# Attention scores of two heads on the two halves of the TensorE array, in a fused attention and mixture kernel

## The chip, the core and the metric

The kernel runs as one program on one core of a Trainium2 chip. The metric is the device time of that program in microseconds (us). The engines are named as the profile names them: PE (TensorE, the matrix array) with PEld for its weight loads, DVE (VectorE), ACT (ScalarE), POOL (GpSimd) and SP (SyncE, which issues the transfers).

## What is computed

Attention with a block mask feeds a first mixture layer, which feeds a second one. The change is in the attention alone, and there almost wholly in `scores = scale * q @ k.T`:

```python
B, H, S, D = 4, 8, 576, 64                  # batches, heads, positions, head width
scores = scale * np.matmul(q, k.transpose(0, 1, 3, 2))
scores = np.where(pos[:, None] // 64 >= pos[None, :] // 64, scores, -1e9)
attn = softmax(scores)                      # max taken off, sum + 1e-9
x = np.matmul(attn, v)                      # heads side by side: (2304, 512)
x = maximum(x @ w1, x @ w2, x @ w3) @ w_out # first mixture layer, d_ff 768
out = sum_e p[:, e] * (maximum(x @ W1[e], 0) @ W2[e])   # second, 4 experts, d_ff 1024
```

All inputs are 32-bit floats, and the products must be more exact than one pass of the array in its rounded 32-bit form (`F32R`) gives. So a factor is held as two parts, the rounded value ("high") and what is left of it ("low"), and several products of parts are summed.

## The kernel before

**Stages.** There are 16 pairs of heads, four to a batch. Batch 0's attention runs by itself; from then on the first mixture layer of batch b (`moe1`, matmuls on line 528) is mixed into the attention of batch b + 1 as filler, and what is left of it runs on after the last scores, until about 530 us. The second mixture layer (lines 883 to 1042) takes the rest of the time and isn't touched by the change.

**Order of the work.** The loop in `program` writes the stages of one head after another (scores, transposes of the probabilities, products with v, filler). The instructions of each engine are then put in order once, when the program is built, by a scheduler that plans with a model of the engines; on the chip every engine takes its own instructions in that fixed order. The `order` fences below show that order.

**Loads and preparation.** `load_pair` (line 89) brings queries and keys of a pair with each head's 64 rows held twice, on partitions 0 to 63 and again on 64 to 127: 2 x 2 x 576 columns. `prep_pair` (line 105) makes the parts. Keys: ACT rounds 1152 columns (line 85), and DVE takes the rounded value off on the lower 64 partitions (line 122), so that `kk` holds high parts on top and low parts below. Queries: ACT scales and rounds 1024 and 128 columns (line 133) into `q1`, DVE forms the low parts `q2` (line 135). POOL clears a 64-column gap in each (line 118). In batch 0 the odd pairs put all this in `spare`.

**Scores.** `scores` (line 163) makes one head's scores in two groups. For query block i (128 queries) the key widths are 128, 256, 384 and 512. A block takes two matmuls of 128 array rows (line 190): `kk` against `q1`, which sums high x high and low x high, and against `q2`. The last 64 queries of both heads make one further block (i = 4, 320 and 256 columns) of four matmuls each. In batches 0 and 1 one short matmul with `corner` (line 195) masks a block; in batches 2 and 3 DVE does (line 204). Then DVE finds the extreme of each row (line 208), ACT takes the exponential (line 215), `normalise` makes reciprocals (lines 223, 224). The scores' PSUM tiles come from `ps_x`, four banks that `tt` (transposes, line 274) and others use too, and `ps_c`.

**Around it.** `turn_probs` transposes probabilities on PE (line 274) and copies them out (DVE or ACT, line 299). In batch 0 the values (line 328) are 32-bit matmuls without parts.

Of the kernel before, what the change touches and what calls it, by code (L numbers as in the profile page):

```python
# [24 lines left out]
def program(tc, q, k, v, w123, w_out, probs, e_w1, e_w2, out):  # L25
    nc = tc.nc

    B, H, D, S = q.shape[0], 2 * q.shape[1], q.shape[2] // 2, q.shape[4]
# [25 lines left out]
    nc.gpsimd.memset(corner[0:1, 0:64], 1e15)  # L54
# [26 lines left out]
    QT, QW = 2 * (S - 64), 2 * S + 64  # L81
    pairs, heads, later, made = {}, {}, [], {}
# [6 lines left out]
    def load_pair(g):  # L89
        b, h0 = divmod(2 * g, H)  # L90

        if g % 2:
            raw = ap_.tile([P, 2, 2, S], F32, name="raw", tag="raw")[:]
        else:
            o = (B - 1) * KD * S
            raw = arena[:, o:o + 4 * S].rearrange("p (n h s) -> p n h s", n=2, h=2)
        for hs in ((0, 1), (1, 2)) if g == 0 else ((0, 2),):
            for n, src in ((1, k), (0, q)):
                nc.sync.dma_start(out=raw[:, n, hs[0]:hs[1]], in_=src[b, h0 // 2, :, hs[0]:hs[1]])

        vraw = ap_.tile([P, 5, 2, D], F32, name="vraw", tag="vraw", bufs=4)
        nc.sync.dma_start(out=vraw, in_=v[b, h0 // 2])
        pairs[g] = dict(raw=raw, vraw=vraw)

    def prep_pair(g):


        raw, vraw = pairs[g]["raw"], pairs[g]["vraw"]
        if g < NPAIR and g % 2:

            spare = mp.tile([P, 2 * QW + 2 * S], F32R, name="spare", tag="hh")
            q1, q2 = spare[:, 0:QW], spare[:, QW:2 * QW]
            kk = spare[:, 2 * QW:].rearrange("x (h s) -> x h s", h=2)
        else:
            q1, q2 = (ap_.tile([P, QW], F32R, name=x, tag=x, bufs=1)[:] for x in ("q1", "q2"))
            kk = ap_.tile([P, 2, S], F32R, name="kk", tag="kk", bufs=1)[:]
        for x in (q1, q2):
            nc.gpsimd.memset(x[:, QT + 64:QT + 128].bitcast(U32), 0)

        def keys(hs):  # L120
            (rounded if g else lambda _, to, x: rounded(nc.vector, to, x))(nc.scalar, kk[:, hs], raw[:, 1, hs])
            nc.vector.tensor_tensor(kk[hi, hs], raw[hi, 1, hs], f(kk[hi, hs]), op=ALU.subtract)

        def queries(hs):
            x = raw[:, 0, hs]
            parts = []
            for to in (q1, q2):
                main = to[:, 0:QT].rearrange("x (h s) -> x h s", h=2)[:, hs]
                tail = to[:, QT:QW].rearrange("x (t s) -> x t s", s=64)[:, 0:3:2][:, hs]
                parts.append((main, tail))  # L130
            srcs = (x[:, :, 0:S - 64], x[:, :, S - 64:S])
            for high, src in zip(parts[0], srcs):
                nc.scalar.activation(high, src, ACTF.Copy, scale=-scale)  # L133
            for high, low, src in zip(*parts, srcs):
                nc.vector.scalar_tensor_tensor(low, src, -scale, f(high), op0=ALU.mult, op1=ALU.subtract)

        if g == 0:
            for h in range(2):
                keys(slice(h, h + 1))
                queries(slice(h, h + 1))  # L140
            yield
        else:
            keys(slice(0, 2))
            yield
            queries(slice(0, 2))
        pairs[g].update(q1=q1, q2=q2, kk=kk)
        if g < NPAIR:
# [6 lines left out]
        pairs[g]["vs"] = vs  # L154
# [3 lines left out]
    GROUPS = [  # L158
        [("x", 512, [(0, 0, P), (2, P, 384)]), ("x", 512, [(3, 0, 512)])],
        [[("x", 512, [(1, 0, 256)])], [("c", 1024, [(4, 192, 576), (1, 768, 256)])]],  # L160
    ]

    def scores(g, grp):
        pair, h = pairs[g // 2], g % 2
        if grp == 0:
            heads[g] = dict(
                p=[None] * 4,
                mn=ap_.tile([P, 5], F32, name="mn", tag="mn", bufs=3),
                sm=ap_.tile([P, 5, 2], F32, name="sm", tag="sm", bufs=3),
            )  # L170
        mn, sm, pt = heads[g]["mn"], heads[g]["sm"][:, :, 0], heads[g]["p"]
        masked = g < 2 * H
        c0 = 3 * grp
        sets = []
        for tag, cols, plan in GROUPS[1][h] if grp else GROUPS[0]:
            st = (ps_x if tag == "x" else ps_c).tile([P, cols], F32, name="st", tag=tag)
            sets.append((st, plan))
            for i, o, w in plan:

                if i == 4:  # L180
                    todo = [(QT + 64 * x, x) for x in range(2)]
                else:
                    todo = [(h * QT // 2 + P * i, h)]
                c = 0
                while c < w:
                    n = min(w - c, 512 - (o + c) % 512)
                    terms = [(part, q0, x) for q0, x in todo for part in ("q1", "q2")]
                    ends = masked and i < 4 and c + n == w
                    for m, (part, q0, x) in enumerate(terms):
                        nc.tensor.matmul(  # L190
                            out=st[:, o + c:o + c + n], lhsT=pair[part][:, q0:q0 + P],
                            rhs=pair["kk"][:, x, c:c + n], start=m == 0, stop=m == len(terms) - 1 and not ends,
                        )
                    if ends:
                        nc.tensor.matmul(  # L195
                            out=st[:, o + w - 64:o + w], lhsT=corner, rhs=corner[:, 0:64], start=False, stop=True
                        )
                    c += n
        c = c0
        done = []  # L200
        for st, plan in sets:
            for i, o, w in plan:
                if i < 4 and not masked:
                    nc.vector.memset(st[lo, o + w - 64:o + w], 1e30)
            mine = [(c + n, *x) for n, x in enumerate(plan)]
            c += len(plan)
            for col, i, o, w in mine:
                nc.vector.tensor_reduce(mn[:, col:col + 1], st[:, o:o + w], axis=AX.X, op=ALU.min)  # L208
            for col, i, o, w in mine:
                x = ap_.tile([P, w], F32, name=f"p{i}", tag=f"p{i}", bufs=2 if i == 4 else 3)  # L210
                if i == 4:
                    pair["p4"] = x
                else:
                    pt[i] = x
                nc.scalar.activation(  # L215
                    x, st[:, o:o + w], ACTF.Exp, bias=mn[:, col:col + 1], scale=-1.0,
                    accum_out=sm[:, col:col + 1],
                )
                done.append((col, x))

        def normalise():
            cs = slice(c0, c)
            nc.vector.tensor_scalar(sm[:, cs], sm[:, cs], 1e-9, None, op0=ALU.add)
            nc.vector.reciprocal(sm[:, cs], sm[:, cs])  # L224
            if g < H:

                if grp == 0 and h == 0:
                    o = 4 * (g // 2) * P
                    pair["rb"] = arena[:, o:o + 4 * P].rearrange("p (i h c) -> p i h c", i=4, h=2)
                rb = pair["rb"][:, 0:3, h] if grp == 0 else pair["rb"][:, 3:4, h]  # L230
                rs = sm[:, c0:c] if grp == 0 else sm[:, c - 1:c]
                nc.gpsimd.tensor_copy(rb, rs.unsqueeze(2).to_broadcast([P, c - c0 if grp == 0 else 1, 64]))
            for col, x in done:
                if g < H and x is not pair.get("p4"):
                    continue
                nc.gpsimd.tensor_scalar(x, x, sm[:, col:col + 1], 1.0, op0=ALU.mult, op1=ALU.mult)  # L236
# [22 lines left out]
    def turn_probs(g, part):  # L259
# [8 lines left out]
        pt = heads[g]["p"] + [pair["p4"]]  # L268
# [42 lines left out]
    def values32(g, part):  # L311


        pair, hd, h = pairs[g // 2], heads[g], g % 2
        eh, vraw = pair["eh"], pair["vraw"]
        own = lo if h == 0 else hi
# [21 lines left out]
        if part == 0:  # L338
            nc.scalar.copy(xf[own, 0:P], hd["pv"][0][own, 0:P])
# [7 lines left out]
        del heads[g]  # L347
# [12 lines left out]
    def values(g, part):  # L360
# [3 lines left out]
        hd, vs, h = heads[g], pairs[g // 2]["vs"], g % 2  # L364
# [23 lines left out]
        own, other = (lo, hi) if h == 0 else (hi, lo)  # L388
# [6 lines left out]
        tmp = ap_.tile([P, 512], F32, name="tmp", tag="tmp", bufs=1)[own, 0:n]  # L395
# [972 lines left out]
```

## Time and profile before

| | |
|---|---|
| three timed runs | 1253.21, 1253.94, 1254.67 us; median 1253.94 |
| span of the profiled execution | 1247.6 us (first to last instruction), 6.3 us under the median |
| PE busy | 1210.9 us, 97% of the span |
| DVE, ACT, POOL busy | 934.0, 516.4, 339.0 us |
| attention | from 0 to about 400 us |

The page's granted TensorE clock is 9 or more tenths of full speed in all 40 slices. PE is the engine with the most work over the whole span; the first 88 us, batch 0, differ from the rest, and so a change is to be weighed stage by stage. Matmul durations in the trace include the time in which a matmul runs out of the array while the next one is already in it; what a matmul costs in a full stretch is the distance from its start to the next one's.

### The profile page before, as it was taken

Reading aid. Unit: us, or ns where it says so; the run is one execution under the profiler, and the core shown is the slowest. Engines: PE = TensorE matmul, PEld = TensorE weight load, DVE = VectorE, ACT = ScalarE, POOL = GpSimd, SP = SyncE. Lnnn points to the kernel's source line nnn. Section 1 sums busy time; section 2 is a strip of 40 time slices with the busy share of each in tenths; the row PEclk is TensorE's granted clock in tenths of the full one; section 3 lists DMA queues with packets and bytes.
Section 4 is the critical chain, followed back from the end, with each engine's and each line's share of the span. In section 5 each row is a group of like instructions: output and inputs, shape, how many; then the busy total and the mean of one; then the engine's idle time right before and its main releaser. Section 6 shows DMA issues by size and latency. Waiting matters only on the chain.

```text
span 1247.6 us, 19748 instructions
## 1 busy us (share of the span) xinstructions
PE 1210.9 (97%) x7433; PEld 1157.6 (93%) x7433; DVE 934.0 (75%) x1720; ACT 516.4 (41%) x1076; POOL 339.0 (27%) x428
## 2 busy tenths in 40 slices
PE   6889998999999999999999999999999999999998
PEld 5668997999999999989999998999999999999998
DVE  8979888666565634378888886758787788586896
ACT  7976767544544421234434441233232222322232
POOL 3648786454344212243333341000000000000000
PEclk9999999999999999999999999999999999999999
DMA  8745475545533488479888865778787887766754
GB/s 320 266 144 194 162 263 167 168 151 156 182 103 118 120 298 293 154 305 336 306 308 297 312 239 169 281 279 317 294 310 308 313 315 289 253 251 235 253 203 178
DMA packets 82644, 299.69 MB, mean 240 GB/s; under 512 B 8748, under 2 KB 18036, under 8 KB 69492
## 3 DMA queue, kind: packets, MB, share of 16 engines
q1 hardware_dynamic: 82548, 298.42, 67.2%
q8 instruction: 59, 0.97, 0.3%
q14 instruction: 37, 0.30, 0.1%
HBM read 215.26 MB, written 83.14 MB: 239 GB/s over the span
## 4 chain that ended last, share of the span: by engine, by line
PE 71%; DVE 13%; DMA 7%; ACT 4%; issue 3%; POOL 2%; SPq 0%; DVEq 0%; ACTq 0%; POOLq 0%
PE m L883 22%; PE m L528 19%; PE o L1042 17%; DMA t<-in_e_w 3%; PE st L190 3%; PE pv L382 2%; PE tt L274 2%; PE m L1042 2%; DMA part<-in_e_w 2%; DVE mn L208 2%; PE o L965 1%; PE o L968 1%; PE o L969 1%; PE pv L328 1%; DVE w L838 1%
## 5 line engine op out<-in xcount | busy, mean ns | idle before, releaser
L528 PE MATMUL m<-xh,wt 128*128 128x288 f32 x1120 | 238.8, 298 | 1.9 <-DVE mt L566 1.6
L883 PE MATMUL m<-t,w 128*128 128x384 f32 x1152 | 228.5, 336 | 0.0
L1042 PE MATMUL o<-hx,w 128*128 128x384 f32 x1176 | 225.8, 337 | 0.0
L1042 PEld LDWEIGHTS o<-hx,w 128*128 128x128 f32 x1176 | 207.9, 188 | 0.0
L883 PEld LDWEIGHTS m<-t,w 128*128 128x128 f32 x1152 | 203.3, 188 | 2.6 <-DVE tmp L903 0.4
L528 PEld LDWEIGHTS m<-xh,wt 128*128 128x128 f32 x1120 | 183.8, 188 | 2.8 <-DVE mt L566 2.0
L883 PE MATMUL m<-b,w 128*128 128x384 f32 x864 | 175.7, 337 | 2.9 <-ACT tmp L908 2.9
L528 PE MATMUL m<-xl,wt 128*128 128x288 f32 x560 | 165.2, 295 | 0.0
L883 PEld LDWEIGHTS m<-b,w 128*128 128x128 f32 x864 | 153.2, 188 | 6.0 <-ACT tmp L908 3.2
L528 PEld LDWEIGHTS m<-xl,wt 128*128 128x128 f32 x560 | 105.2, 188 | 0.3
L903 DVE TENSOR_TENSOR tmp<-m,tmp 128x384 f32<-128x384 f32 x144 | 77.8, 549 | 18.7 <-PE m L883 18.3
L236 POOL TENSOR_SCALAR p<-p,sm 128x128 f32<-128x128 f32 (+4 forms) x112 | 73.7, 674 | 46.5 <-DVE sm L224 17.5
L528 PE MATMUL m<-hh,wo 128*128 128x288 f32 x384 | 81.3, 299 | 2.7 <-ACT arena L577 1.3
L215 ACT ACTIVATE p<-st,mn 128x128 f32<-128x128 f32 (+3 forms) x144 | 78.4, 554 | 8.3 <-DVE mn L208 7.8
L1013 ACT CAST hx<-hq 128x768 fp32r<-128x768 f32 x49 | 40.5, 836 | 99.2 <-PE o L1042 76.1
L190 PE MATMUL st<-kk,q 128*128 128x128 f32 (+4 forms) x336 | 70.3, 339 | 7.5 <-ACT q L133 5.3
L965 PE MATMUL o<-w,hh 128*128 128x512 f32 x192 | 74.7, 391 | 0.8 <-ACT hh L943 0.5
L968 PE MATMUL o<-w,hh 128*128 128x512 f32 x192 | 74.7, 390 | 0.0
L969 PE MATMUL o<-w,hl 128*128 128x512 f32 x192 | 74.1, 390 | 0.0
L838 POOL TENSOR_TENSOR w<-part,w 128x512 fp32r<-128x512 f32 x32 | 48.8, 1547 | 88.7 <-ACT w L836 71.3
L566 DVE TENSOR_TENSOR mt<-m,mt 128x288 f32<-128x288 f32 x96 | 43.1, 452 | 39.1 <-PE m L528 38.6
L208 DVE TENSOR_REDUCE mn<-st 128x1 f32<-128x128 f32 (+3 forms) x144 | 66.4, 504 | 2.8 <-PE st L195 2.5
(173 smaller groups left out, 2182.0 us busy)
## 6 DMA issues: line engine op xcount, KB each, us to landing
w<-kb SPq DMA_DIRECT2D x55, 1024.0 KB, 5.5
w<-ka SPq DMA_DIRECT2D x30, 1792.0 KB, 7.5
ka<-w SPq DMA_DIRECT2D x16, 1792.0 KB, 6.7
wt<-held SPq DMA_DIRECT2D x54, 512.0 KB, 4.1
kb<-part SPq DMA_DIRECT2D x16, 1024.0 KB, 6.9
kb<-w SPq DMA_DIRECT2D x16, 768.0 KB, 5.2
arena<-in_w SPq DMA_DIRECT2D x18, 512.0 KB, 4.1
wo<-held SPq DMA_DIRECT2D x12, 768.0 KB, 4.5
```

The source lines that it names most:

```text
L190: nc.tensor.matmul(out=st[:, o + c:o + c + n], lhsT=pair[part][:, q0:q0 + P], rhs=pair["kk"][:, x, c:c + n], start=m == 0, stop=m == len(t ...
L208: nc.vector.tensor_reduce(mn[:, col:col + 1], st[:, o:o + w], axis=AX.X, op=ALU.min)
L215: nc.scalar.activation(x, st[:, o:o + w], ACTF.Exp, bias=mn[:, col:col + 1], scale=-1.0, accum_out=sm[:, col:col + 1],)
L236: nc.gpsimd.tensor_scalar(x, x, sm[:, col:col + 1], 1.0, op0=ALU.mult, op1=ALU.mult)
L528: nc.tensor.matmul(out=out_, lhsT=w, rhs=x, start=m == 0, stop=m == n - 1)
L838: eng.tensor_tensor(w[:, a:b, 1], raw[:, a:b], f(w[:, a:b, 0]), op=ALU.subtract)
L883: ins = nc.tensor.matmul(out=m, lhsT=a, rhs=b, start=start and n == 0, stop=stop and n == 3 * KH - 1, skip_group_check=True,)
L903: nc.vector.tensor_tensor(t, x, y, op=ALU.add)
L965: ins = nc.tensor.matmul(out=o, lhsT=hh[:, ts], rhs=wh, start=i == 0, stop=False)
L968: nc.tensor.matmul(out=o, lhsT=hh[:, ts], rhs=wl, start=False, stop=False)
L969: nc.tensor.matmul(out=o, lhsT=hl[:, ts], rhs=wh, start=False, stop=i == G - 1)
L1042: nc.tensor.matmul(out=o, lhsT=a, rhs=b, start=start and m == 0, stop=stop and m == 2, skip_group_check=True,)
```

## The change

Queries and keys of a pair are now held once: head 0 on partitions 0 to 63, head 1 on 64 to 127. A score matmul uses half of the array's rows (64 of 128), and the matmuls of the two heads are written alternately, into different PSUM tiles. Since high and low parts can no longer be stacked on the array's rows, a block takes three matmuls a head (high x high, high x low, low x high; `TERMS`); low x low is left out. The last 64 queries lie in the same columns for both heads, with zeros laid in by the host, so that their block is three matmuls of all 128 rows (line 176). Scores come in three stages a pair; the loop goes over pairs; `qk` has two buffers where `q1`, `q2`, `kk` had one.

```diff
-            raw = ap_.tile([P, 2, 2, S], F32, name="raw", tag="raw")[:]
+            raw = ap_.tile([P, S + QW], F32, name="raw", tag="raw")[:]
...
+        nc.sync.dma_start(out=raw[:, 0:S], in_=k[b, m])
+        nc.sync.dma_start(out=raw[:, S:], in_=q[b, m])
...
+            spare = ap_.tile([P, 2 * (S + QW)], F32R, name="qk", tag="qk", bufs=2)
-        for x in (q1, q2):
-            nc.gpsimd.memset(x[:, QT + 64:QT + 128].bitcast(U32), 0)
...
-            nc.vector.tensor_tensor(kk[hi, hs], raw[hi, 1, hs], f(kk[hi, hs]), op=ALU.subtract)
+        rounded(nc.scalar if n else nc.vector, ks[0], raw[:, 0:S])
+        nc.vector.tensor_tensor(ks[1], raw[:, 0:S], f(ks[0]), op=ALU.subtract)
+        yield
+        nc.scalar.activation(qs[0], raw[:, S:], ACTF.Copy, scale=-scale)
+        nc.vector.scalar_tensor_tensor(qs[1], raw[:, S:], -scale, f(qs[0]), op0=ALU.mult, op1=ALU.subtract)
...
+    STEPS = [
+        (("x", 512), ("x", 512), [(0, 0, 0, P), (2, P, P, 384)]),
+        (("x", 512), ("x", 512), [(3, 0, 0, 512)]),
+        (("x", 512), ("c", 1024), [(1, 0, 768, 256)]),
     ]
+    TERMS = ((0, 0), (0, 1), (1, 0))
...
-                    terms = [(part, q0, x) for q0, x in todo for part in ("q1", "q2")]
...
+            for m, (x, y) in enumerate(TERMS):
+                for h in range(2):
+                    nc.tensor.matmul(
+                        out=views[h], lhsT=qs[x][own[h], P * i:P * i + P], rhs=ks[y][own[h], 0:w],
+                        start=m == 0, stop=m == 2 and not masked,
+                    )
...
+        if step == 2:
+            view = st[1][:, 192:768]
+            for c, n_ in ((0, 320), (320, 256)):
+                for m, (x, y) in enumerate(TERMS):
+                    nc.tensor.matmul(
+                        out=view[:, c:c + n_], lhsT=qs[x][:, QT:QW], rhs=ks[y][:, c:c + n_],
+                        start=m == 0, stop=m == 2,
+                    )
...
-            todo = [ta, s0, tb, s1, pp, va, pp, vb]
+        todo = [ta[0], s0, tb[0], s1, va[0], pp, vb[0], ta[1], s2, tb[1], va[1], pp, vb[1]]
```

**Order on PE, in the third batch.** `st` is a scores tile, `m` the filler's, `tt` a transpose's. Before, one head's scores of blocks 0, 2 and 3:

```order
L528 MATMUL m_3532<-xl_2461,wt_3530 128x288
L528 MATMUL m_3532<-xh_2460,wt_3530 128x288
L274 MATMUL tt_3622<-ident_58,p2_3272 128x128
L190 MATMUL st_3649<-kk_3338,q1_3336 128x128
L190 MATMUL st_3649<-kk_3338,q2_3337 128x128
L190 MATMUL st_3649<-kk_3338,q1_3336 128x384
L190 MATMUL st_3649<-kk_3338,q2_3337 128x384
L190 MATMUL st_3654<-kk_3338,q1_3336 128x512
L190 MATMUL st_3654<-kk_3338,q2_3337 128x512
```

Now, of a pair in the same batch, where `st_3789` and `st_3871` are head 0's and `st_3790` and `st_3872` head 1's:

```order
L510 MATMUL m_3772<-xh_2386,wt_3722 128x288
L161 MATMUL st_3789<-qk_3549 128x128 x3
L161 MATMUL st_3789<-qk_3549 128x384 x3
L161 MATMUL st_3790<-qk_3549 128x128 x3
L161 MATMUL st_3790<-qk_3549 128x384 x3
L510 MATMUL m_3821<-xh_2386,wt_3819 128x288
...
L161 MATMUL st_3871<-qk_3549 128x512 x3
L510 MATMUL m_3889<-xh_2386,wt_3887 128x288
...
L161 MATMUL st_3872<-qk_3549 128x512 x3
```

The three terms of a block stand together, first all of one head, then all of the other; the alternation of the source is kept in few places.

**Order on DVE, in batch 0.** The preparation of one later pair and the copy of transposed probabilities, `eh`, behind it. Before:

```order
L135 SCALAR_TENSOR_TENSOR q_634<-arena,q_633 128x1024
L135 SCALAR_TENSOR_TENSOR q_634<-arena,q_633 128x2x64
L122 TENSOR_TENSOR kk<-arena,kk 64x1152
L299 COPY eh<-tt 128x512
L223 TENSOR_SCALAR sm<-sm 128x3
```

Now:

```order
L118 TENSOR_TENSOR qk<-raw,qk 128x576
L444 SCALAR_TENSOR_TENSOR arena<-arena 128x512
L121 SCALAR_TENSOR_TENSOR qk<-raw,qk 128x640
L203 TENSOR_SCALAR sm<-sm 128x3
L204 RECIPROCAL sm<-sm 128x3
L282 COPY eh<-tt 128x512
```

The preparation of a pair is two instructions of 576 and 640 columns where it was three of 1152, 1024 and 128.

**Order on DVE, at the start of the program.** Before:

```order
L135 SCALAR_TENSOR_TENSOR q_132<-arena,q_131 128x512
L135 SCALAR_TENSOR_TENSOR q_132<-arena,q_131 128x64
L208 TENSOR_REDUCE mn<-st 128x1 x4
L122 TENSOR_TENSOR spare<-raw,spare 64x1152
L208 TENSOR_REDUCE mn<-st 128x1 x2
```

Now:

```order
L121 SCALAR_TENSOR_TENSOR qk<-arena,qk 128x640
L118 TENSOR_TENSOR spare<-raw,spare 128x576
L121 SCALAR_TENSOR_TENSOR spare<-raw,spare 128x640
L118 TENSOR_TENSOR qk<-arena,qk 128x576
L189 TENSOR_REDUCE mn<-st 128x1 x6
```

The first reductions of scores now stand behind the preparation of the second pair and the keys of the third.

## Rows read from the trace of the kernel before

**Rows 1.** The page's first line: span and instructions of the profiled execution.

```profile
span 1247.6 us, 19748 instructions
```

**Rows 2.** Stretches: length, each engine's busy us (instructions), granted clock, DMA share, GB/s.

```profile
core 0: us, PE busy (x) PEld busy (x) DVE busy (x) ACT busy (x) POOL busy (x), PEclk, DMA share, GB/s
0.00:88.00 88.00, 68.97 (x384) 51.68 (x384) 75.56 (x150) 72.99 (x191) 44.40 (x71) 0.96 0.73 257
88.00:240.00 152.00, 144.36 (x1052) 136.56 (x1052) 127.79 (x291) 102.36 (x250) 105.47 (x137) 1.00 0.57 190
240.00:520.00 280.00, 277.90 (x2073) 274.70 (x2072) 155.79 (x387) 115.02 (x282) 95.90 (x156) 1.00 0.54 172
```

**Rows 3.** PE's waits, 0 to 88 us: total us, times, longest.

```profile
PE st L190 <- ACT q L133: 5.3, 1, 5.3
PE pv L328 <- ACT eh L299: 4.8, 2, 2.5
PE tt L274 <- DVE eh L299: 2.3, 1, 2.3
```

**Rows 4.** The chain that ended last, by line, 0 to 88 us.

```profile
by line: PE pv L328 12.4%; DVE mn L208 10.0%; issue 8.4%; DVE q L135 5.9%; PE st L190 5.5%; DVE kk L122 4.8%; ACT p L215 4.5%; DVE spare L135 4.4%; DMA arena<-in_q 3.9%; DVE eh L299 3.5%; PE tt L274 3.5%; DVE spare L122 3.3%; ACT spare L85 
```

**Rows 5.** Timeline, DVE and PE around 50 us: start, length, instructions, idle before.

```profile
47.63 2.50 DVE L135 SCALAR_TENSOR_TENSOR q<-arena,q 128x1024 fp32r<-128x1024 f32 x2
50.16 2.60 DVE L122 TENSOR_TENSOR kk<-arena,kk 64x1152 fp32r<-64x1152 f32 x1
52.79 0.69 DVE L299 COPY eh<-tt 128x512 f32<-128x512 f32 x1
...
53.54 0.65 PE L274 MATMUL tt<-ident,p 128*128 128x128 f32 x4 [2.27 <-DVE eh L299]
```

**Rows 6.** Timeline of PE in full stretches, at 304 and 313 us.

```profile
304.72 0.52 PE L190 MATMUL st<-kk,q 128*128 128x256 f32 x3
305.08 0.60 PE L274 MATMUL tt<-ident,p 128*128 128x128 f32 x4
305.44 1.29 PE L190 MATMUL st<-kk,q 128*128 128x128 f32 x6
306.57 0.29 PE L528 MATMUL m<-xh,wt 128*128 128x288 f32 x1
306.70 0.29 PE L528 MATMUL m<-xl,wt 128*128 128x288 f32 x1
...
313.01 1.46 PE L190 MATMUL st<-kk,q 128*128 128x320 f32 x10
314.30 0.29 PE L528 MATMUL m<-hl,wo 128*128 128x288 f32 x1
```

**Rows 7.** Timeline of PE, two scores of 128 columns and a corner.

```profile
49.74 0.42 PE L190 MATMUL st<-spare 128*128 128x128 f32 x2
49.99 0.20 PE L195 MATMUL st<-corner 128*128 128x64 bf16 x1
```

**Rows 8.** Busy time of DVE's line 122 alone, 0 to 88 us.

```profile
0.00:88.00 88.00, 9.99 (x7) 0.96 0.73 257
```

**Rows 9.** Busy time of DVE's line 135 alone, 0 to 88 us.

```profile
0.00:88.00 88.00, 11.57 (x14) 0.96 0.73 257
```

**Rows 10.** Groups by line and shape, 0 to 88 us: count, busy us, mean ns.

```profile
L547 DVE TENSOR_TENSOR xl<-xf,xh 128x576 fp32r<-128x576 f32 x4 | 3.3, 830 | 0.0
L135 DVE SCALAR_TENSOR_TENSOR q<-arena,q 128x512 fp32r<-128x512 f32 x2 | 1.4, 692 | 0.2 <-ACT q L133 0.2
L85 ACT CAST kk<-arena 128x1152 fp32r<-128x1152 f32 x2 | 2.3, 1147 | 0.0
L546 ACT CAST xh<-xf 128x576 fp32r<-128x576 f32 x4 | 2.7, 678 | 0.3 <-DVE xf L358 0.3
```

**Rows 11.** The first 10 us, as in rows 2.

```profile
0.00:10.00 10.00, 4.66 (x19) 3.77 (x19) 5.58 (x12) 3.91 (x10) 1.27 (x12) 1.00 0.82 292
```

**Rows 12.** The chain in order of time: the first reductions.

```profile
8.16 0.68 DVE mn L208 x2
```

More of the change, by code (lines that the diff above doesn't have):

```diff
@@ L79, in program @@
     lo, hi, both = slice(0, 64), slice(64, 128), slice(0, P)
-    QT, QW = 2 * (S - 64), 2 * S + 64
-    pairs, heads, later, made = {}, {}, [], {}
+    own = (lo, hi)
+    QT, QW = S - 64, S + 64
+    pairs, later, made = {}, [], {}
     def rounded(engine, to, x):
@@ L153, in prep_pair @@
         nc.gpsimd.tensor_tensor(vs[:, :, :, 64:128], src, f(vh), op=ALU.subtract)
[L154 to L160, printed above, removed]
-    ]
[L163 to L169, printed above, removed]
-            )
[L171 to L178, printed above, removed]
+        pairs[n]["vs"] = vs
@@ L180, in scores @@
                 if i == 4:
-                    todo = [(QT + 64 * x, x) for x in range(2)]
+                    pair["p4"] = to
                 else:
[L183 to L186, printed above, removed]
-                    terms = [(part, q0, x) for q0, x in todo for part in ("q1", "q2")]
[L188 to L214, printed above, removed]
+                    pair["p"][h][i] = to
@@ L233, in normalise @@
-            for col, x in done:
-                if g < H and x is not pair.get("p4"):
+                    to = pair["rb"][:, 0:2].rearrange("p i h c -> p h i c")
+                    rs = sm[:, cs].rearrange("p (h i) -> p h i", h=2).unsqueeze(3).to_broadcast([P, 2, 2, 64])
+                else:
+                    to = pair["rb"][:, step + 1]
+                    rs = sm[:, COLS[step]:COLS[step] + 2].unsqueeze(2).to_broadcast([P, 2, 64])
+                nc.gpsimd.tensor_copy(to, rs)
+            for c, i, x in done:
+                if n < NPAIR and i < 4:
@@ L267, in turn_probs @@
         el = eh[:, LAST + 2:]
-        pt = heads[g]["p"] + [pair["p4"]]
+        pt = pair["p"][h] + [pair["p4"]]
         for n in PARTS[part]:
@@ L311, in values32 @@
     def values32(g, part):
-        pair, hd, h = pairs[g // 2], heads[g], g % 2
+        pair, h = pairs[g // 2], g % 2
+        hd = pair.setdefault(h, {})
         eh, vraw = pair["eh"], pair["vraw"]
-        own = lo if h == 0 else hi
+        mine = own[h]
         both_v = [vraw[:, j].rearrange("p h d -> p (h d)") for j in range(5)]
@@ new lines, in program @@
+    for n in range(NALL):
+        b, d = divmod(n, NPAIR)
+        ahead = n + 2 < NALL
+        prep = prep_pair(n + 2) if ahead else iter(())
+        g = 2 * n
+        ta, tb, va, vb = [
+            [(fn, g + h, part) for h in range(2)] for fn in (turn_probs, values) for part in range(2)
+        ]
+        s0, s1, s2 = [(scores, n + 1, i) if n + 1 < NALL else (None,) for i in range(3)]
+        pp = (next, prep, None)
+        todo = [ta[0], s0, tb[0], s1, va[0], pp, vb[0], ta[1], s2, tb[1], va[1], pp, vb[1]]
+        for m, st in enumerate(todo):
+            if d == NPAIR - 1 and m == 7:
+                moe1_inputs(b, range(KD - 1))
+            stage(*st)
+            if b == 0 and st is vb[0] and n:
+                weigh(n - 1, made["pv"])
+            if d == NPAIR - 1 and m == len(todo) - 1:
+                if b == 0:
+                    weigh(n, made["pv"])
```

179 lines of the change are left out of this document (82 added, 97 removed).

## The prediction

> **What bounds the kernel now.** I first read the line with the span [rows 1] and the table of stretches [rows 2]. From 240 to 520 us PE is busy 277.9 of 280 us while DVE has 155.8: there every nanosecond on PE is on the path, and DVE, ACT and the loads are cover. From 88 to 240 us PE is busy 144.4 of 152 us, so 7.6 us are stalls. From 0 to 88 us (batch 0) PE is busy 69.0 of 88, DVE 75.6 and ACT 73.0: no engine is full, work passes from one to the next, and 19.0 us are stalls of PE. PE's waits say for whom [rows 3]: 5.3 us is the start, before the first queries are ready, and nearly all the rest ends with ACT's or DVE's copy of transposed probabilities (line 299). The chain of waits in that stretch [rows 4] says why these are late: DVE's preparation of later pairs (lines 135 and 122) is 5.9 + 4.8 + 4.4 + 3.3 = 18.4% of it, 16.2 us. One place shows it plainly [rows 5]: DVE spends 5.1 us from 47.6 us on a later pair's query and key parts, only then makes the copy, and PE sits idle 2.27 us for it. After 520 us nothing of the change is left.
>
> So there are two accounts: what the change takes off DVE and ACT counts in the first 88 us and for some of the 7.6 us after them; what it adds to PE counts nearly in full from 88 us on.
>
> **PE's scores.** What a matmul costs is the distance between starts in a full stretch [rows 6]. Three of 256 columns: 304.72 to 305.08, 0.12 us each. One head's blocks 0, 2 and 3, two matmuls each of 128, 384 and 512 columns: 305.44 to 306.57, 1.13 us. Four of 320 and six of 256: 313.01 to 314.30, 1.29 us, of which 0.72 for the six and 0.57 for the four. A pair now costs 2 x (1.13 + 0.24) for the two heads and 0.57 + 0.48 for the shared last block: 3.79 us. After the change each head has three matmuls where it had two, each on half of the array's rows and over the same columns. No row of this trace shows a half-array matmul, so I bound it. If the two heads never overlap, a pair costs 1.5 x 2.74 + 0.75 x 1.05 = 4.90 us, 1.11 more. If they always do, 0.5 x 4.11 + 0.79 = 2.84 us, 0.95 less. Between the two I choose by the order. The source writes the heads alternately, but the scheduler has put the three terms of one head together and then those of the other, often with filler between (the third-batch fence). In the trace PE starts its instructions in the order of the program; only the last matmul of one head and the first of the other can then lie beside each other. That order has 32 such neighbours after the first filler matmul and 26 before it (half of these in pair 0, the one place that still alternates). Each can hide at most a short matmul, and two of 128 columns took 0.25 us [rows 7]; I take 0.10 each, and for the whole 0 to 0.125. At 88 us, 254 of the 384 score matmuls are still to come, 10.6 pairs: 10.6 x 1.11 - 3.2 = **+8.6 us** on a full PE. Before 88 us: 5.4 x 1.11 - 2.6 = +3.4 us of work in a stretch that has stalls.
>
> **Changes between half and whole array.** Filler, transposes and values still use 128 rows, so PE goes back and forth: 118 changes after the first filler matmul, 29 before it. The trace has none. The low end is zero: four transposes between two kinds of other matmuls take 0.36 us and delay neither neighbour [rows 6], and there is nothing that a change could save. For the high end, a filler matmul is in the array 0.29 us while the next starts after 0.13 [rows 6]; if each change waits until the array is empty, it costs the other 0.16. I take 0.05, nearer to the changes of kind that do occur: 118 x 0.05 = **+5.9 us**, and 29 x 0.05 = +1.5 before 88 us. The ends are 0 and +18.9.
>
> **DVE and ACT.** In the first 88 us lines 122 and 135 take 9.99 and 11.57 us for six pairs [rows 8, 9], 21.6 in all, 3.6 a pair. Afterwards a pair has a subtraction of 576 columns on all partitions, as line 547 now (0.83 us), and a query part of 640, by the 512 of line 135 (0.69) 0.87: 1.70 a pair, 10.2 for six, 53% less [rows 10]. ACT's rounding of keys falls from 1.15 us to 0.68. If the 16.2 us on the chain shrink by 53%, 8.6 us go; the most that can go is 19.0 - 5.3 = 13.7 us of stalls, since then PE is full. What is late next is PE, which has 3.4 + 1.5 us more to do there. Against this stands a new queue at the start: the first reductions of scores, which free PE's score tiles, now stand on DVE behind the second pair's parts and the third pair's keys, the eighth transfer of SP's queue. These eight transfers are 2.5 MB (128 rows of 576 or 640 columns of 4 bytes each); at the 292 GB/s of the first 10 us [rows 11] that is 8.7 us, and with rounding and subtraction the reductions start at about 10.5 us where they start at 8.16 now [rows 12]. Some of that preparation stood behind them and is then already done; I charge 1 us (0 to 2.3). First stretch: 3.4 + 1.5 - 8.6 + 1 = **-2.7 us**, with ends at -10.3 (all stalls gone, the other charges nothing) and +2.9 (half of the 8.6, and 2.3).
>
> From 88 to 240 us DVE loses another 1.9 us a pair for some four pairs, 7.6 of 127.8 us busy. POOL, also loaded there (105.5 us), loses only short fills. Of the 7.6 us of PE stalls I let 3 go: **-3 us** (0 to -7.6).
>
> The rest I cost at nothing. Loads of queries and keys halve and hide behind work as they do now; if they were late, it would show at the start, charged above. The three stages a pair drop one of four `normalise` groups. Both heads need score tiles at once out of the same four banks: a half that waits for its bank holds up all of PE behind it, with filler ahead of it in the order as cover; uncovered it would cost some 0.5 us a pair.
>
> Sum: 8.6 + 5.9 - 2.7 - 3 = +8.8 us on the span of 1247.6, so 1256.4. The median of the timed runs is 6.3 us above the span; with that **1263 us**.
>
> **Rivals.**
>
> Changes are free. The same sum without the 5.9 and the 1.5 gives +1.4 us: 1255 us, no change. For it: no change of kind costs PE anything in the trace. Against: none of these is a change of array rows.
>
> Every change empties the array. At 0.16 us, 118 changes are 18.9 us instead of 5.9, and 29 add 3.1: +24.9 us, 1279. For it: a whole-array matmul needs the very rows that the half one may still be in, and the tail of 0.16 us is there to be waited for. Against: the trace has no such wait between any two matmuls. The Trainium skill ("TensorEngine Tiling (Array Packing)", Key Properties) says that changing the tiling mode, not just the tile, drains TensorE, with no price; no run here shows it, and by it this rival would be the forecast.
>
> The other side: DVE and ACT give back more than PE loses. It needs free changes and all stalls gone, 13.7 us in the first stretch and 7.6 in the second: 8.6 + 3.4 - 13.7 - 7.6 = -9.3, 1245 us. It decides from about 15 us of stalls removed. For it: the copies that PE waits for stand right behind preparation that halves. Against: part of these waits is the round trip of scores, exponentials and transposes, which stays.
>
> The chip lays the heads side by side in spite of the order: -0.95 x 10.6 = -10.1 us in place of +8.6, 1244 us with the rest of the sum as it is. For it: the row halves don't share data. Against: three terms of one head use the same rows and stand in front of the other head's. The Trainium skill ("TensorE: Matmul & The Clock Gate", LDWEIGHTS) has weight loads take as long for few rows as for 128, P/1.2 ns; two 128-column matmuls at 0.25 us [rows 7], no faster than 256-column ones, agree. By it 24 loads bind a pair at an estimated 2.57 us in place of 2.06, and this rival comes to 1250 us.
>
> **How the numbers follow.** The forecast, a partly paid change of mode, 0.42; emptying at each change (above 1270) 0.18; free changes 0.18, all within 0.2% of before; DVE and ACT win 0.16; side by side 0.06. That is slower 0.60, the same 0.18, faster 0.22, where the same means within 0.2% (1251.4 to 1256.4), about what a measurement of this kernel can tell from no change. The range reaches from 1247 (most of the stalls gone) to 1279 (each change at the full price) and leaves out about 2 in 10.
>
> **What would show it.** Right: in full stretches three 512-column half matmuls of one head start about 0.23 us apart, one behind the other; PE busy time in scores rises by about a quarter after 88 us; the stalls of the first stretch fall below 12 us and line 299 no longer heads PE's waits. The distance from a half matmul to the whole one behind it, less that between two whole ones, is the price of a change: 0.05 for the forecast, 0 and 0.16 for its rivals. Wrong: three half matmuls of one head in less time than two whole ones had, starts of the two heads within a few ns of each other, or stalls before 88 us that stay at 19 us.

## The result, and the profile after

| | before | after |
|---|---|---|
| median of the timed runs | 1254.16 us (1253.21 to 1254.67) | 1262.35 us (1261.56 to 1263.75) |
| ratio | | 1.0073, 95% interval 1.0057 to 1.0090 |
| span of the trace | 1247.6 us | 1259.8 us |
| to the first filler matmul | 88.1 us | 85.9 us |
| first to last filler matmul | 430.2 us | 442.3 us |
| the rest | 729.3 us | 731.6 us |

The kernel is 8.2 us slower. The forecast was 1263, slower, and its three terms for the stage of the filler came to +11.5 us (8.6 + 5.9 - 3), which the trace gives as +12.1; for the stage before it -2.7 us, which the trace gives as -2.2. So far the sum holds. The experiments show that it holds in part by errors that cancel: the change between half and whole array costs about four times what was charged, and the heads lie side by side far more than was allowed for. Of all runs below one, of the ten of the kernel grouped by head, took 2395.27 us; the ratios leave it out, and without it that kernel's median would be 1247.23 us.

The stage limits in the table are starts of the filler's matmuls. In the trace of after, by the line's first and last start (count, shortest, median and longest ns, then first and last start in us):

```profile
L510 PE MATMUL m<-xh,wt x1120: 288/295/404, 85.9 to 508.7; 128*128 128x288 f32 x187
L510 PE MATMUL m<-hh,wo x384: 288/295/403, 186.5 to 528.2; 128*128 128x288 f32 x192
```

The stretches of after, in the columns of [rows 2]:

```profile
0.00:88.00 88.00, 74.80 (x433) 58.20 (x433) 66.30 (x136) 69.15 (x188) 37.95 (x56) 1.00 0.63 211
88.00:240.00 152.00, 151.75 (x1079) 139.55 (x1078) 118.49 (x273) 97.57 (x240) 98.86 (x127) 1.00 0.53 173
240.00:520.00 280.00, 278.55 (x2024) 265.07 (x2023) 149.05 (x368) 109.61 (x269) 90.57 (x146) 1.00 0.49 158
```

DVE's busy time falls by 9.3 us in the first stretch and again by 9.3 in the second. From 88 to 240 us PE now has 0.25 us of stalls where it had 7.6. It is full, with 1079 matmuls in this stretch instead of 1052. The mean granted clock of the first stretch is 1.00, where it was 0.96 [rows 2]. PE's waits in the first 88 us, which answer to [rows 3]:

```profile
PE st L161 <- ACT qk L120: 5.2, 1, 5.2
PE st L161 <- ACT p L196: 2.6, 2, 2.4
PE pv L312 <- ACT eh L282: 2.1, 3, 1.0
```

The start is what it was. The copy of transposed probabilities (line 299, now 282) made PE wait 4.8 us in one of the rows of before and makes it wait 2.1 in the row of after. Stalls in the first 88 us go from 19.0 to 13.2 us.

What PE pays is seen at any place where one head's block of 512 columns stands alone between fillers. A stretch of half-array matmuls between two whole-array ones is called a visit to the half array below. Timeline of PE in after, and then that of the run `e2_whole_rows` below, which has the same three matmuls on all 128 rows (start, length, instructions):

```profile
274.08 0.29 PE L510 MATMUL m<-xh,wt 128*128 128x288 f32 x1
274.31 0.96 PE L161 MATMUL st<-qk 64*128 64x512 f32 x3
275.20 0.40 PE L510 MATMUL m<-xh,wt 128*128 128x288 f32 x1
275.44 0.30 PE L510 MATMUL m<-xl,wt 128*128 128x288 f32 x1
```

```profile
241.46 0.87 PE L161 MATMUL st<-qk 128*128 128x512 f32 x3
242.16 0.30 PE L510 MATMUL m<-xh,wt 128*128 128x288 f32 x1
```

A filler matmul is followed after 0.13 us by the next one [rows 6], but by a half-array one only after 274.31 - 274.08 = 0.23. The three take 0.89 us where whole ones take 0.70, and the first filler behind them holds the next up for 0.24 instead of 0.13. One visit to the half array costs 0.10 + 0.19 + 0.11 = 0.40 us, 0.20 for each change. In the trace of after PE visits the half array 59 times between the first and the last filler matmul: 23 us, if all cost as much. An estimate from the starts of all 59, against the spacing of the same matmuls on all 128 rows (0.23 us for 512 columns), gives a little less. The 47 visits without blocks of both heads cost 17.0 us, 0.36 each; the 12 with blocks of both take 2.8 us less than their matmuls would one behind the other. That is about 21 us for the changes and 7 us saved by the overlap.

### The profile page after: what moved, and what is told of

Same layout as the page of the kernel before. It is cut to its first block, busy times and chain, and to the rows that moved or that the text cites. A ratio compares the mean times of both kernels' runs of the same rounds, so it can differ in the third digit from the quotient of the medians.

```text
span 1259.8 us, 19862 instructions
## 1 busy us (share of the span) xinstructions
PE 1236.3 (98%) x7529; PEld 1168.7 (93%) x7529; DVE 909.8 (72%) x1668; ACT 504.4 (40%) x1058; POOL 319.0 (25%) x393
## 4 chain that ended last, share of the span: by engine, by line
PE 87%; DVE 4%; DMA 4%; ACT 2%; POOL 1%; issue 1%; SPq 0%; ACTq 0%; POOLq 0%
PE m L859 25%; PE m L510 23%; PE o L1018 16%; PE st L161 4%; PE o L941 3%; PE tt L257 3%; PE o L944 3%; PE o L945 3%; PE pv L366 2%; PE m L1018 2%; DMA kb<-part 1%; PE st L176 1%; DVE mn L189 1%; DMA w<-ka 1%; PE pv L312 1%
## 5 line engine op out<-in xcount | busy, mean ns | idle before, releaser
L510 PE MATMUL m<-xh,wt 128*128 128x288 f32 x1120 | 246.6, 301 | 0.0
L219 POOL TENSOR_SCALAR p<-p,sm 128x128 f32<-128x128 f32 (+4 forms) x112 | 67.3, 616 | 110.6 <-DVE sm L204 76.5
L196 ACT ACTIVATE p<-st,mn 128x128 f32<-128x128 f32 (+2 forms) x144 | 78.1, 550 | 37.0 <-DVE mn L189 36.3
L189 DVE TENSOR_REDUCE mn<-st 128x1 f32<-128x384 f32 (+4 forms) x144 | 68.8, 513 | 6.2 <-PE st L167 4.4
L161 PE MATMUL st<-qk 64*128 64x384 f32 (+3 forms) x336 | 63.8, 360 | 7.6 <-ACT qk L120 5.2
```

The costliest lines, as they stand in the source:

```text
L161: nc.tensor.matmul(out=views[h], lhsT=qs[x][own[h], P * i:P * i + P], rhs=ks[y][own[h], 0:w], start=m == 0, stop=m == 2 and not masked,)
L189: nc.vector.tensor_reduce(mn[:, c:c + 1], x, axis=AX.X, op=ALU.min)
L196: nc.scalar.activation(to, x, ACTF.Exp, bias=mn[:, c:c + 1], scale=-1.0, accum_out=sm[:, c:c + 1],)
L219: nc.gpsimd.tensor_scalar(x, x, sm[:, c:c + 1], 1.0, op0=ALU.mult, op1=ALU.mult)
L510: nc.tensor.matmul(out=out_, lhsT=w, rhs=x, start=m == 0, stop=m == n - 1)
```

## The experiments

Every comparison with before is with runs of it on the same chip; the median of these lies between 1252.2 and 1252.9 us. Stages as in the table above, in us, from one trace each; two traces of the same kernel differ by up to 1.1, 1.7 and 2.5 us in the three stages:

| run | median, us | ratio to before (95%) | to first filler | filler | rest |
|---|---|---|---|---|---|
| before, traced again | | | 88.8 | 430.6 | 731.8 |
| after, traced again | | | 87.0 | 444.0 | 730.0 |
| corner on half the rows | 1260.65 | 1.0063 (1.0043 to 1.0082) | 92.2 | 434.1 | 732.3 |
| scores on all rows | 1252.39 | 0.9995 (0.9984 to 1.0006) | 87.0 | 432.4 | 730.7 |
| preparation twice | 1269.93 | 1.0131 (1.0114 to 1.0148) | 94.9 | 443.0 | 731.0 |
| heads held in turn | 1255.03 | 1.0014 (1.0003 to 1.0026) | 88.7 | 435.3 | 728.5 |
| grouped, in turn | 1249.27 | 0.9977 (0.9965 to 0.9988) | 86.5 | 436.1 | 729.3 |
| grouped, by head | 1247.40 | 0.9955 (0.9944 to 0.9966) | 84.5 | 432.0 | 730.4 |
| reductions first | 1265.53 | 1.0113 (1.0096 to 1.0130) | 90.3 | 443.9 | 729.4 |
| grouped and reductions first | 1252.91 | 0.9999 (0.9990 to 1.0009) | 90.9 | 431.2 | 729.9 |

### The price of a change, by itself

```diff
-    out=st[:, o + w - 64:o + w], lhsT=corner, rhs=corner[:, 0:64], start=False, stop=True
+    out=st[:, o + w - 64:o + w], lhsT=corner[lo], rhs=corner[lo, 0:64], start=False, stop=True
```

> The kernel before with one thing changed: the 64 matmuls that add the mask corner (batches 0 and 1) use 64 of the array's rows instead of 128. Work, order of stages, preparation and result are those of before; PE now changes between whole and half array 128 times, 46 of them after the first filler matmul. Theory from the trace of after (each change holds PE up by about 0.09 us at the change and 0.10 us at the next start, some 0.2 us for a corner in and out beyond what a whole-array corner takes): 23 corners x 0.2 = +4.6 us where PE is full, and for the 41 corners before it between nothing and 8 us: 1259 to 1267. Forecast's price (0.05 a change): +2.3 and at most 4: 1256 to 1260. Rival, changes are free: 1254.

Measured: 1260.65 us, 7.7 us over before, with nothing changed but the array rows of 64 short matmuls. Of it about 4 us lie before the first filler matmul and about 4 in the stage of the filler. Two scores of 256 columns, a corner and two filler matmuls, in before and then in this run:

```profile
95.52 0.40 PE L190 MATMUL st<-kk,q 128*128 128x256 f32 x2
95.76 0.20 PE L195 MATMUL st<-corner 128*128 128x64 bf16 x1
95.80 0.51 PE L528 MATMUL m<-xh,wt 128*128 128x288 f32 x2
96.14 0.29 PE L528 MATMUL m<-xl,wt 128*128 128x288 f32 x1
```

```profile
100.26 0.40 PE L190 MATMUL st<-kk,q 128*128 128x256 f32 x2
100.59 0.20 PE L195 MATMUL st<-corner 64*128 64x64 bf16 x1
100.72 0.53 PE L528 MATMUL m<-xh,wt 128*128 128x288 f32 x2
101.09 0.29 PE L528 MATMUL m<-xl,wt 128*128 128x288 f32 x1
```

From the first score to the last filler matmul: 0.62 us before, 0.83 with the half corner, +0.21 for two changes around a single matmul. In a visit of several matmuls there is also the second one of the visit, which starts late; hence 0.40 above. That changes are free is refuted, and 0.05 is too low by a factor of two to four. The Trainium skill ("TensorEngine Tiling (Array Packing)", Key Properties) says that changing the mode drains TensorE. The rows agree that each change is paid for, and give the price; that the array is empty in between they don't show, for the filler starts at 100.72 us, 0.07 before the end that the trace gives the corner (100.59 + 0.20).

### No changes, no overlap

```diff
-    out=views[h], lhsT=qs[x][own[h], P * i:P * i + P], rhs=ks[y][own[h], 0:w],
+    out=views[h], lhsT=qs[x][:, P * i:P * i + P], rhs=ks[y][:, 0:w],
...
-    out=views[h][:, w - 64:w], lhsT=corner[own[h]], rhs=corner[own[h], 0:64],
+    out=views[h][:, w - 64:w], lhsT=corner, rhs=corner[:, 0:64],
```

> The changed kernel with its preparation, loads, stages and number of score matmuls, but each score and corner matmul uses all 128 rows, so that a head's scores are the sum of both heads' (the separation of the heads is left out). No change between half and whole array is left, and nothing can lie side by side. Theory from the trace of after: the changes cost about 22 us after 88 us and the overlap saves about 8: 1262 - 22 + 8 = 1248. Forecast's prices (changes 5.9 + 1.5, overlap 3.2 + 2.6): 1261. Rival, changes are free and overlap is worth 8 or more: 1270.

Measured: 1252.39 us, 10 us below after and level with before. The stage of the filler takes 432.4 us, 10 less than after and 2.2 more than before. This run separates the accounts. Against before, each head's blocks have three score matmuls where they had two, one behind the other: PE's stalls from 88 to 520 us fell from 9.7 us [rows 2] to 3.4, so 2.2 us more in all means 8.5 us more work. Against after: 59 visits at up to 0.40 us, 23 us, are gone, and 10 us are gained, so what the side-by-side halves saved in after is about 11 us (1.7 us of stalls came back). That is a remainder, and the mean granted clock from 88 to 240 us is 0.99 here and 1.00 in after, some 1.5 us of it. The expectation, from the trace of after, said 22 and 8; the sum over the visits above, 21 and 7.

```profile
88.00:240.00 152.00, 150.17 (x1099) 144.98 (x1099) 118.39 (x278) 99.45 (x249) 100.24 (x129) 0.99 0.53 174
240.00:520.00 280.00, 278.48 (x2074) 275.24 (x2073) 149.16 (x365) 108.95 (x267) 89.70 (x145) 1.00 0.51 163
```

### What the lighter preparation is worth

```diff
+        rounded(nc.scalar if n else nc.vector, ks[0], raw[:, 0:S])
+        nc.vector.tensor_tensor(ks[1], raw[:, 0:S], f(ks[0]), op=ALU.subtract)
...
+        nc.scalar.activation(qs[0], raw[:, S:], ACTF.Copy, scale=-scale)
+        nc.vector.scalar_tensor_tensor(qs[1], raw[:, S:], -scale, f(qs[0]), op0=ALU.mult, op1=ALU.subtract)
```

> The changed kernel with each pair's key and query parts made twice over (the same four instructions again, same values): DVE and ACT have about as many columns of preparation as before the change. Nothing else is changed. If the relief of DVE and ACT is what took PE's stalls away, they return: 5 to 9 us before the first filler matmul and 3 to 8 us after it, 1270 to 1279. Rival, PE is the bound all along and the relief bought nothing: 1262.

Measured: 1269.93 us. The first filler matmul comes at 94.9 us instead of 85.9 (87.0 in the second trace of after): 8 to 9 us. To the first filler matmul, in after and then in this run, and this run's first wait:

```profile
0.00:85.90 85.90, 72.70 (x418) 56.47 (x419) 64.97 (x133) 68.13 (x184) 37.95 (x56) 1.00 0.65 217
```

```profile
0.00:94.90 94.90, 77.05 (x417) 58.38 (x418) 76.50 (x148) 76.93 (x197) 39.61 (x56) 0.95 0.57 192
```

```profile
PE st L165 <- ACT qk L124: 7.2, 1, 7.2
```

Of the 9 us, 4.6 are stalls of PE (17.8 instead of 13.2) and 4.4 a longer time for the same matmuls, at a mean granted clock of 0.95 instead of 1.00. Of the stalls, 2.0 lie at the very start: the first wait, the last line, is 7.2 us where after has 5.2 and before 5.3, since here the first pair too is prepared twice, one time behind the other. So this run doesn't give the 8.6 us that the forecast had put on the preparation: 2.6 us of stalls are left for the later pairs, and how much of the clock's part belongs to them is open.

The stage of the filler is as long as in after, 443.0 us, with DVE busier than before the change from 88 to 240 us and PE's stalls still at 1.7 us of 152:

```profile
88.00:240.00 152.00, 150.32 (x1052) 135.92 (x1053) 129.42 (x284) 108.38 (x265) 100.73 (x126) 1.00 0.52 166
```

So the stalls that vanished there were not taken away by the relief of DVE and ACT. That a slower PE lets the other engines keep up would explain it, and `e1_half_corner`, with the preparation and the order of before, points that way: with only the half corners added its stalls in this stretch are 5.4 us instead of 7.6. How much the new order of the stages adds was not tried.

```profile
88.00:240.00 152.00, 146.63 (x1019) 135.47 (x1018) 124.79 (x283) 102.61 (x248) 104.64 (x138) 0.99 0.56 189
```

### Holding the heads side by side

```diff
-            for m, (x, y) in enumerate(TERMS):
-                for h in range(2):
-                    nc.tensor.matmul(
+        def behind(**kw):
+            if last:
+                with tc.issue_after(last.pop().ins):
+                    last.append(nc.tensor.matmul(**kw))
+            else:
+                last.append(nc.tensor.matmul(**kw))
...
+            for m, (x, y) in enumerate(TERMS):
+                for h in (0, 1):
+                    behind(
```

> The changed kernel with the score matmuls of the two heads held in the alternating order in which they are written (each is queued behind the one before it). 92 changes between half and whole array after the first filler matmul instead of 118. Theory from the trace of after: 26 changes fewer at 0.19 us = -5, and all blocks overlapped instead of a part of them, -10 to -12: 1245 to 1249, faster than both kernels. If weight loads of the two halves can't overlap, 128- and 256-column blocks gain nothing: about 1254. Rival, the halves don't run side by side at all: 1258 to 1262.

Measured: 1255.03 us, a miss: 7 us better than after, not 13 to 17. PE visited the half array 46 times instead of 59, and its work in the stage of the filler (the stage less its stalls) fell from 440.6 to 428.8 us. But PE now waits more, 23 us instead of 13 before the first filler matmul, and 6.5 instead of 1.7 in the stage of the filler. From 0 to 530 us:

```profile
PE st L164 <- ACT p L206: 7.3, 4, 4.8
PE st L164 <- ACT qk L120: 5.6, 1, 5.6
PE tt L267 <- ACT p L206: 4.7, 4, 3.1
```

The first of these ends with the exponentials, which read a score tile and so free it. It fits that an order that is held makes everything behind it wait until both heads' banks are free; this was not tried by itself.

The time is close to the 1254 us of the rival in which the weight loads of the two halves can't overlap. The rows speak against it: six matmuls of 256 columns, three of each head, take 0.55 us in this run, as long as three of one head in after (the last line of each shows where the next matmul starts).

```profile
247.84 0.38 PE L164 MATMUL st<-qk 64*128 64x256 f32 x1
247.85 0.62 PE L162 MATMUL st<-qk 64*128 64x256 f32 x5
248.39 0.42 PE L186 MATMUL st<-qk 128*128 128x320 f32 x1
```

```profile
259.00 0.61 PE L161 MATMUL st<-qk 64*128 64x256 f32 x3
259.55 0.71 PE L176 MATMUL st<-qk 128*128 128x320 f32 x3
```

The next two leave batch 0 to the scheduler, and hold the first matmul of a stage behind what is traced before it on PE, which was meant to leave fewer visits. They differ only in the order of the loops over terms and heads:

```diff
+                with tc.issue_after(prev.ins) if n >= NPAIR else nullcontext():
+                    last.append(nc.tensor.matmul(**kw))
+            elif n >= NPAIR:
+                last.append(tc.keep_in_program_order(nc.tensor.matmul(**kw)))
```

```diff
-            for m, (x, y) in enumerate(TERMS):
-                for h in (0, 1):
+            for h in (0, 1):
+                for m, (x, y) in enumerate(TERMS):
```

> The changed kernel; from batch 1 on the score matmuls of a stage are held in the alternating order in which they are written, and the first of them behind the work traced before it on PE; batch 0 is left to the scheduler. 78 changes between half and whole array after the first filler matmul (118 after the change, 92 where the order alone was held). Theory (0.19 us a change, overlap of all blocks, and waits for two banks at once costing some 5 us as in the run with the order held throughout): 1246 to 1251. If the waits grow with the grouping and eat the gain: 1255 or more.

> As the grouped kernel, with the same 78 changes, but within a stage the three matmuls of a block of head 0 are held ahead of the three of head 1. Theory, PE starts a matmul on the idle half out of the order of the program, so that the order within a visit to the half array doesn't matter: within 1.5 us of the grouped kernel. The forecast's step, only the last matmul of one head and the first of the other can lie beside each other: 8 to 10 us slower than the grouped kernel.

Measured: 1249.27 us in turn and 1247.40 by head. PE visits the half array 39 times in both. A visit with both heads' blocks of 512 columns, grouped in turn and then grouped by head (the first matmul of a visit has a line of its own):

```profile
302.12 0.50 PE L165 MATMUL st<-qk 64*128 64x512 f32 x1
302.13 0.96 PE L163 MATMUL st<-qk 64*128 64x512 f32 x5
303.02 0.41 PE L523 MATMUL m<-xh,wt 128*128 128x288 f32 x1
```

```profile
295.16 0.50 PE L165 MATMUL st<-qk 64*128 64x512 f32 x1
295.17 0.96 PE L163 MATMUL st<-qk 64*128 64x512 f32 x5
296.06 0.40 PE L523 MATMUL m<-xh,wt 128*128 128x288 f32 x1
```

Six matmuls take 0.90 us, as long as three of one head alone in after (0.89), and the second matmul of the visit starts 0.01 us after the first: the second head costs nothing. That holds by head too, where the program has three of head 0 and only then three of head 1. So the order of the three terms of a block within a visit doesn't matter, and the forecast's step that only neighbours of different heads can overlap is refuted. It matters how far apart the heads stand, though. With the blocks of 128 and 384 columns in one visit, grouped by head, each block of head 0 is followed by the same block of head 1, and the twelve matmuls take 1.06 us; in after, with both blocks of head 0 first, they take 1.34 (shown below, at 267.52 us):

```profile
288.52 0.32 PE L165 MATMUL st<-qk 64*128 64x128 f32 x1
288.53 1.12 PE L163 MATMUL st<-qk 64*128 64x128 f32 x11
289.58 0.40 PE L523 MATMUL m<-xh,wt 128*128 128x288 f32 x1
```

The grouped kernel by head is 1.9 us faster than the one in turn, a little more than the 1.5 us of the expectation. Why is not shown: in the traces its stage of the filler is 4 us shorter, with 4 us of stalls instead of 9, but the trace of the kernel in turn is that of its slowest run (1253.71 us), with a granted clock of 0.98 instead of 1.00 from 88 to 240 us. The kernel grouped by head beats before by 0.45% and after by 1.2%.

### The queue at the start

```diff
-        nc.vector.tensor_tensor(ks[1], raw[:, 0:S], f(ks[0]), op=ALU.subtract)
+        low = nc.vector.tensor_tensor(ks[1], raw[:, 0:S], f(ks[0]), op=ALU.subtract)
+        if n in (1, 2):
+            tc.keep_in_program_order(low)
```

and the same for the queries' low part.

> The changed kernel; on DVE the low parts of the second and third pair are held behind the reductions of scores that are traced before them, so that the first reductions no longer stand behind the preparation of later pairs. 118 changes after the first filler matmul as before. In the changed kernel the first reduction starts at 11.8 us, in the kernel before at 8.2. If that queue costs what the forecast charged, 1 us, the first filler matmul comes about 1 us earlier: 1261 to 1262. If the whole 3.7 us is on the path: 1258 to 1259. If later pairs' preparation is then late instead: 1263 or more.

> The kernel grouped by head (78 changes, 1247.4 us) together with the reductions held first on DVE. The two act in different stages, the one after the first filler matmul, the other before it, so that the gain of the run with the reductions held first should be added: 1243 to 1247, and 1247 if that run shows no gain.

Measured: 1265.53 and 1252.91 us, both worse than without the hold (1262.35 and 1247.40). DVE's first reductions in after and then in `e9_reduce_first`:

```profile
11.81 2.61 DVE L189 TENSOR_REDUCE mn<-st 128x1 f32<-128x128 f32 x6
```

```profile
8.66 2.61 DVE L193 TENSOR_REDUCE mn<-st 128x1 f32<-128x128 f32 x6 [2.62 <-PE st L171]
```

They start 3.2 us earlier, and the first filler matmul comes 3 to 4 us later. Taking the queue away in this way gained nothing; the time is that of the expectation's last case, later pairs' preparation that comes late. What the queue costs by itself is not shown, for the hold moved the parts of both next pairs, and which of the moved instructions makes the loss wasn't tried apart.

### The two kernels traced again

> The kernel before, unchanged, for a second trace of it. The trace that the prediction was read from has a span of 1247.6 us, under the span of every timed run of it that followed (1248.5 to 1253.0). If that trace was of a fast execution, this one has a span near 1251, and its stages differ from the first one's by the granted clock alone; its three stages (to the first filler matmul, the filler, the rest) should be about 88, 432 and 731 us.

> The changed kernel, unchanged, on the same chip as the other runs of this group: a span near 1260 us, stages near 86, 442 and 731 us, and the same 59 visits of PE to the half array after the first filler matmul.

Measured: spans of 1251.2 and 1261.0 us, +9.8. All timed runs lie 1.7 to 1.9 us over their spans, of both kernels. So the trace that the forecast was read from, 1247.6 us, belongs to an execution of about 1249.4 us, faster than any timed run of before. The stages of the second trace are 0.7, 0.4 and 2.5 us longer; its mean granted clock is 0.992, that of the first 0.997. Of the +12.2 us between the first two traces, 2.3 lie in the rest, which the change doesn't touch; in the second pair the rest is 1.8 us shorter.

## Why the prediction was right, point by point

**The result.** 1263 forecast, 1262.35 measured; +8.8 us forecast on the span, +8.2 measured between the medians, +12.2 and +9.8 between the spans of the two pairs of traces. The direction and the limits of the stages were right; that the number is right to 1 us is luck, as the terms show.

**From span to median.** The 6.3 us added at the end were 1.8 us that lie around every span and 4.5 us by which that one execution was faster than the median. It was right to add them, but only 1.8 of them are time outside the span.

**Scores, +8.6 us.** The size came out, the way didn't. One behind the other they cost 8.5 us of work more in `e2_whole_rows`; the forecast had 11.8 for that, then took off 3.2 for the neighbours that could overlap. In after the halves saved 7 to 11 us. The step that only the last matmul of one head and the first of the other can lie beside each other failed: PE runs the heads side by side across several matmuls of one visit, though the program has all three of one head first. In after a visit with both heads' 128- and 384-column blocks takes less than the sum:

```profile
267.52 1.41 PE L161 MATMUL st<-qk 64*128 64x128 f32 x12
268.86 0.40 PE L510 MATMUL m<-xh,wt 128*128 128x288 f32 x1
```

Twelve matmuls in 1.34 us, though the program has six of head 0 ahead of six of head 1; grouped block by block they take 1.06. Where a head's block stands alone, as the 512 columns at 274 us, nothing can overlap. The rival that laid the heads side by side in spite of the order was right in part: 7 to 11 us of the 22 between its -10.1 and the +11.8 of no overlap.

**Changes, +5.9 us.** Mis-sized, and the forecast's own high end (0.16 each, 18.9 us) is under what was measured: 0.18 to 0.20 each, 59 visits, 21 to 23 us. The high end counted one wait until the array is empty. The rows show a late start at the change and a second late start behind it: 0.10 and 0.11 us around a lone filler. The rival of the emptied array was nearer in price, though what the rows show is two waits of some 0.10 us and not one of 0.16; its 1279 us came out wrong because it kept the overlap at 3.2 us and let only 3 us of stalls go.

**Stalls from 88 to 240 us, -3 us.** 7.4 us went, but not for the reason given: with the preparation doubled they stay away. If a busier PE hid them, as the half corners suggest, this gain is part of what PE lost.

**The first 88 us, -2.7 us.** -2.2 in the first pair of traces, -1.8 in the second. In the first pair PE's stalls fell by 5.8 us, where 8.6 less 1 was forecast, and its busy time before the first filler matmul rose by 3.6 us (69.1 to 72.7), where 3.4 + 1.5 was forecast: two misses of one to two us that cancel. The granted clock was 0.96 in before and 1.00 in after (0.92 and 0.98 in the second traces), which the forecast had not reckoned with and which no run separates. What the preparation alone is worth is open too (4.6 us of stalls come back when it is doubled, 2.0 of them at the start), and the charge for the queue at the start (+1) was not borne out.

**What would show it.** Stalls of the first stretch were to fall below 12 us and fell to 13.2; line 299 no longer heads PE's waits, as said. PE's time in scores, by starts in the stage of the filler, rose by 31% (42.6 to 56.0 us), where a quarter was said. In the trace of after the second and third half matmul of 512 columns of one head stand 0.23 us apart (the first two 0.34), one behind the other, and the third and the filler behind it 0.32: by the text's measure a change costs 0.09, between its 0.05 and 0.16, but this measure misses the second late start. Starts of the two heads lie within 0.01 us in the grouped runs: by the text's own sign, the step on the overlap was wrong.

**Sum.** 8.6 + 5.9 - 3 = 11.5 stood for the stage of the filler. The runs give, roughly, +8.5 (three matmuls for two) - 11 (overlap) + 23 (changes) - 8 (stalls covered) = +12.5, and the traces +12.1 to +13.4; the split between overlap and changes is only good to some 4 us. Against the forecast's 11.8, -3.2, 5.9 and -3, the last three of these were off by 4 to 17 us, and they cancelled.

## What to carry to other kernels

A visit to half the array costs about 0.40 us here, and within a visit the second half is free where both heads stand block by block. So halves pay where both heads' matmuls stand in one unbroken visit (0.90 us for six of 512 columns), and lose where a scheduler scatters them between whole-array work: look at the built order, count the visits, and hold the group together. And where a forecast agrees with the result, test its terms all the same: here undoing one part at a time showed three wrong sizes behind a right sum.

## What was not expected of the hardware

- PE started matmuls on the idle half ahead of earlier ones of the program that were waiting for the busy half: six of 512 columns by head in 0.90 us, as in turn. This reaches only so far: with six of one head ahead of six of the other, twelve took 1.34 us instead of 1.06.
- A change between half and whole array costs on both sides of it, 0.10 us before and about as much behind, also for a single matmul of 64 columns (+0.21 us in and out).
- Weight loads don't bind a visit: grouped, six matmuls of 512 columns need no more time than three. The Trainium skill ("TensorE: Matmul & The Clock Gate", LDWEIGHTS) gives one load of 128 columns as P/1.2 ns, whatever the rows; six one behind the other would be an estimated 0.64 us. In a visit with both heads' 256 columns, grouped by head, the six loads are done within 0.42 us and the first two start 0.01 us apart, so the loads of the two halves overlap:

```profile
246.69 0.18 PEld L165 LDWEIGHTS st<-qk 64*128 64x128 f32 x1 [0.16 <-issue]
246.70 0.41 PEld L163 LDWEIGHTS st<-qk 64*128 64x128 f32 x5
```
